# Attention and two MLPs on one core: two sets of query and key buffers in one sequence of all pairs

## The chip, the cores and the metric

The kernel runs on one core of one Trainium2 chip. The metric is device time in microseconds (us); a run's time is that of its one core. The program has five engines with a queue each: TensorE (PE in the profile, its weight loads PEld), VectorE (DVE), ScalarE (ACT), GpSimd (POOL) and SyncE (SP), which issues DMAs.

## The reference

Three parts follow one another, all in fp32. `q`, `k`, `v` have 4 batches, 8 heads, 576 positions of 64 values.

```python
scores = (q @ k.T) / 8, masked where block_i < block_j      # blocks of 64 positions
attn = softmax(scores);  x = (attn @ v), heads side by side    # 2304 tokens x 512
h = x @ w_in1                                                  # 512 -> 2048
g = h if h >= 1, 0 if h <= -1, else (h + 1) ** 2 / 4
x = g @ w_out1                                                 # 2048 -> 512
h = x @ w_in2;  out = (h * cos(h)) @ w_out2                     # the same sizes
```

## The kernel before

**Numbers.** A product in TensorE's float32r keeps fewer bits than fp32, so most operands are split into a high part (`rounded`, line 152, or a ScalarE copy) and the rest (`rest`, line 155), and three products stand for one. Weights are scaled and rounded bit by bit when they come in (`w_convert`, lines 163 to 222), the result is kept in on-chip slots, and all but the first `w_in` are stored to DRAM (`w_store`, line 143) and fetched again when they are next used (`w_fetch`, line 146).

**Attention.** Work goes by pairs of heads, 16 in all (4 batches of 4). A pair has five units, tiles of 128 queries (the last of 64). `load` (line 273) brings K, Q and V of a pair. `prep` (line 296) transposes K or Q on TensorE, in two parts each, and fills the tiles Q, K and L (high parts, low parts, and a zero half). `scores` (line 350) multiplies, takes the maximum on VectorE and the exponential on ScalarE; `scores_tail` (line 406) does so for the last unit. `p_trans` (line 452) transposes the probabilities into PT, `pv` (line 483) multiplies by V. After a pair's last unit its 576 columns go to DRAM (`x1d`, line 528).

**The MLPs.** Tokens go in half-blocks of 512 (the last has 256). For each half-block and layer there are 16 steps, one for each 128 columns of the hidden layer: `mm1` (line 597, 12 products into the PSUM tile `h`), `act` (line 614, the activation as a chain of operations over several engines), and two steps later `mm2` (line 661, 12 products into `a`). The first half-block needs the first batch, the second half-block the second batch too, and so on; `x_load` (line 569) brings x from `x1d`.

**Order.** Functions are generators that yield after every piece of work. `at(d, fn)` puts an operation d ticks later, and a tick passes with every piece (lines 95 to 104). First attention runs alone (`a0`): batch 0 and the first pair of batch 1, with eight PSUM banks and two sets of Q, K, L and of raw K and Q, the second set in a pool `spare`; it divides by the softmax sum after PV (`late`). Then `zipped` (line 758) mixes: for each piece of the MLP it emits `rates` pieces of the remaining 11 pairs (`a1`), for 48 steps, which are three half-blocks of layer 1. There attention has one set of Q, K, L and three PSUM banks, and `h` has one bank; all four `prep` parts of a pair stand ahead of its first unit (line 549), and POOL divides the probabilities. The rest of layer 1 and all of layer 2 follow, with four banks for `h`.

A planner takes these pieces in the order in which they were emitted and sets the order on each engine's queue at build, by a model of the times; on the chip each queue runs in its fixed order, and an instruction that waits holds what is behind it. SP's queue carries every DMA: loads of K, Q, V and weights, stores and fetches of weights, stores and loads of x.

In `load`, K and Q wait for raw tiles that `prep` has read, V for one of two tiles that `pv` has read. Weights of layer 1's `w_out` go round in `RING` = 5 slots.

Of the kernel before, what the change touches and what calls it, by code (L numbers as in the profile page):

```python
# [32 lines left out]
def attn_moe_moe_kernel(ctx: ExitStack, tc: tile.TileContext, q, k, v, w_in1, w_out1, w_in2, w_out2, out):  # L33
    nc = tc.nc
# [30 lines left out]
    one = const.tile([128, 1], F32, name="one")  # L65
# [12 lines left out]
    def consts():  # L78
        make_identity(nc, ident)
        nc.vector.memset(mk_l[:, 0:64], 1.0)  # L80
        nc.vector.memset(mk_l[:, 64:128], 0.0)
        nc.vector.memset(mk_r, 0.0)
        for i, m in enumerate(MASK_PARTS):
            nc.vector.memset(mk_r[32 * i:32 * i + 1, :], m)
        nc.vector.memset(floor_, FLOOR)
        nc.vector.memset(one, 1.0)
        nc.vector.memset(magic, MAGIC)
        nc.vector.memset(hpi, 0.5 * math.pi)
# [54 lines left out]
    def w_store(layer, f, which, t):  # L143
        nc.sync.dma_start(out=wd[layer, f, which], in_=t.rearrange("p a n -> p (a n)").bitcast(F32))
# [86 lines left out]
    def spare(name, shape, dtype):  # L231
        return P.spare.tile(shape, dtype, name=name + "s", tag=name + "s")

    def attn_pools(stack):
        sb = lambda nm, bufs: stack.enter_context(tc.tile_pool(name=nm, bufs=bufs, side="right"))
        P.v, P.pt, P.xs, P.sm = sb("v", 2), sb("pt", 2), sb("xs", 1), sb("sm", 4)
        P.raw, P.p = sb("qkr", 1), sb("p", 3)
        qk = sb("qk", 1)
        own = lambda name, shape, dtype: qk.tile(shape, dtype, name=name)
        P.qk = []  # L240
        for get in (own, spare):
            Q = [get(f"Q{h}", [128, S + 64], F32R) for h in range(2)]
            K = [get(f"K{h}", [128, S], F32R) for h in range(2)]

            L = [get(f"L{h}", [128, S], F32R) for h in range(2)]
# [14 lines left out]
    def attention(pairs, TL, late=False, sets=1):  # L260


        raws, probs, pts, xst, rs, dens = {}, {}, {}, {}, {}, {}
# [6 lines left out]
        def p_tile(u, h):  # L270
            return P.p.tile([128, S], F32, name=f"P{h}", tag=f"P{h}")

        def load(b, p):
            ts = []
            for src, nm in ((k, "rk"), (q, "rq"), (v, "rv")):
                if src is not v and pairs.index((b, p)) % sets == 1:
                    t = spare(nm, [128, NI, 2, D], F32)
                else:
                    t = (P.v if src is v else P.raw).tile([128, NI, 2, D], F32, name=nm, tag=nm)
                for h in range(2):  # L280
                    nc.sync.dma_start(
                        out=t[:, 0:LAST, h, :],
                        in_=src[b, 2 * p + h, 0:128 * LAST, :].rearrange("(t p) d -> p t d", p=128),
                    )
                P.loaded = nc.sync.dma_start(
                    out=t[0:TAIL, LAST], in_=src[b, 2 * p:2 * p + 2, 128 * LAST:S, :].rearrange("h p d -> p h d")
                )
                ts.append(t)
            raws[b, p] = ts
            if sets == 1 or (b, p) != pairs[0]:  # L290
                load_weights(loaded[0] + 1, len(wq) // 2)

        def qk_of(b, p):
            return P.qk[pairs.index((b, p)) % sets]

        def prep(b, p, which, part):
            t = raws[b, p][which]
# [52 lines left out]
        def scores(u, hs):  # L350
# [4 lines left out]
            o = ps_tile()[:, 0:nk * len(hs)].rearrange("p (h n) -> p h n", h=len(hs))  # L355
            qs = slice(128 * i, 128 * i + 128)
            mm = lambda o, l, r, **kw: nc.tensor.matmul(out=o, lhsT=l, rhs=r, skip_group_check=True, **kw)  # L357
            for c, h in enumerate(hs):
                mm(o[:, c], Q[h][:, qs], K[h][:, 0:nk], start=(c == 0), stop=False)
                mm(o[:, c], Q[h][:, qs], L[h][:, 0:nk], start=False, stop=False)  # L360
            for c, h in enumerate(hs):
                mm(o[:, c, nk - 64:nk], mk_l, mk_r, start=False, stop=True)
            if hs[0] == 0:
                dens[u] = [P.sm.tile([128, 2], F32, name=nm, tag=nm) for nm in ("m", "den", "r")]
            m, den, r = dens[u]
            if hs[-1] == 1:
                del dens[u]

            def top():
                nc.vector.tensor_reduce(  # L370
                    out=m[:, hs[0]:hs[-1] + 1], in_=o, axis=AX.X, op=ALU.max, negate=True
                )

            def exp():
                pr = p_tile(u, hs[0])[:, 0:nk * len(hs)].rearrange("p (h n) -> p h n", h=len(hs))
                for c, h in enumerate(hs):
                    probs[u, h] = pr[:, c]
                    e = nc.scalar.activation(  # L378
                        out=pr[:, c], in_=o[:, c], func=ACTF.Exp, bias=m[:, h:h + 1], accum_out=den[:, h:h + 1]
                    )  # L380
                if b == 0:
                    P.act = e

            def norm():
                ds = (0, 1) if late else hs
                if late and hs[-1] == 0:
                    return
                c = slice(ds[0], ds[-1] + 1)
                nc.vector.tensor_scalar(out=den[:, c], in0=den[:, c], scalar1=1e-9, scalar2=None, op0=ALU.add)
                nc.vector.reciprocal(out=r[:, c], in_=den[:, c])  # L390
                for h in ds:
                    if late:
                        rs[u, h] = r[:, h:h + 1]
                        continue
                    pr = probs[u, h]
                    nc.gpsimd.tensor_scalar(  # L396
                        out=pr, in0=pr, scalar1=r[:, h:h + 1], scalar2=1.0, op0=ALU.mult, op1=ALU.mult
# [5 lines left out]

        tails = {}

        def scores_tail(u, c):
# [19 lines left out]
            def exp():  # L426
                pr = p_tile(u, 0)
# [7 lines left out]
            def norm():  # L435
# [5 lines left out]
                if late:  # L441
# [41 lines left out]
        def pv(u):  # L483
            b, p, i = u
            V = raws[b, p][2]
# [16 lines left out]
            if late:  # L502
# [8 lines left out]
            def out_():  # L511
# [4 lines left out]
                if late:  # L516
# [17 lines left out]
        load(*pairs[0])  # L534
        if sets == 2:
            load(*pairs[1])
        yield "loaded"
        two = sets == 2
        for x in range(n + TL + 1):
# [3 lines left out]
            heads = lambda u: [] if u is None else [(0, 1)] if u[2] < 2 else [(0,), (1,)]  # L543
            S_ = [(scores, u, hs) if u[2] < LAST else (scores_tail, u, hs[0]) for hs in heads(u)]
            T_ = [(p_trans, t, hs) for hs in heads(t)]
            V_ = [(pv, w)] if w else []
            pre = []
            if u and u[2] == 0 and (not two or x == 0):
                pre = [(prep, *u[:2], which, part) for which in range(2) for part in range(2)]
            post = []  # L550
            if u and two and 1 <= u[2] <= 4 and pairs.index(u[:2]) + 1 < len(pairs):
                post = [(prep, *pairs[pairs.index(u[:2]) + 1], (u[2] - 1) // 2, (u[2] - 1) % 2)]
            if pre:
                order = pre + T_ + V_ + S_
            else:
                order = S_[:1] + T_[:1] + S_[1:] + T_[1:] + V_ + post
            for fn, *a in order:
                fn(*a)
                yield fn.__name__
# [330 lines left out]
```

## Time and profile before

| what | value |
|---|---|
| median of 3 runs | 1123.7 us (1123.4 to 1125.97) |
| profiled execution | 1123.27 us |
| its span in the profile | 1121.5 us |
| mean granted clock of TensorE | 0.967 |
| busy: PE, PEld, DVE, ACT, POOL | 1052.1, 850.4, 627.6, 560.3, 546.9 us |
| moved by DMA | 200.35 MB, 179 GB/s |

The span runs from the first instruction to the last; the execution's time has 1.8 us more around it. Busy time is the time in which an engine works on an instruction. Attention alone fills the span up to about 84 us, the mix lasts to about 590, the rest of layer 1 to about 730, layer 2 to the end.

### The profile page before, as it was taken

Reading aid. Unit: us, or ns where it says so; the run is one execution under the profiler, and the core shown is the slowest. Engines: PE = TensorE matmul, PEld = TensorE weight load, DVE = VectorE, ACT = ScalarE, POOL = GpSimd, SP = SyncE. Lnnn points to the kernel's source line nnn. Section 1 sums busy time; section 2 is a strip of 40 time slices with the busy share of each in tenths; the row PEclk is TensorE's granted clock in tenths of the full one; section 3 lists DMA queues with packets and bytes.
Section 4 is the critical chain, followed back from the end, with each engine's and each line's share of the span. In section 5 each row is a group of like instructions: output and inputs, shape, how many; then the busy total and the mean of one; then the engine's idle time right before and its main releaser. Section 6 shows DMA issues by size and latency. Waiting matters only on the chain.

```text
span 1121.5 us, 17067 instructions
## 1 busy us (share of the span) xinstructions
PE 1052.1 (94%) x5912; PEld 850.4 (76%) x5912; DVE 627.6 (56%) x1187; ACT 560.3 (50%) x1253; POOL 546.9 (49%) x609
## 2 busy tenths in 40 slices
PE   9988898989999978999959999999999999999998
PEld 7766676666776756777747789978888888888897
DVE  7876848467545376546615653354454454454464
ACT  7887748567545366445524433243343343343343
POOL 2325957577656447648608975322223323322332
PEclk9998998999998997999979999999999999999999
DMA  5687326557636475536794679822542542442353
GB/s 126 179 264 215 116 77 237 183 174 250 204 108 199 124 248 177 193 103 217 266 336 155 222 262 367 324 90 101 170 143 94 167 134 98 150 145 97 113 188 132
DMA packets 144374, 200.35 MB, mean 179 GB/s; under 512 B 65184, under 2 KB 106144, under 8 KB 144288
## 3 DMA queue, kind: packets, MB, share of 16 engines
q1 hardware_dynamic: 144288, 199.26, 53.9%
q8 instruction: 47, 0.77, 0.3%
q14 instruction: 39, 0.32, 0.1%
HBM read 150.47 MB, written 48.76 MB: 178 GB/s over the span
## 4 chain that ended last, share of the span: by engine, by line
PE 42%; POOL 2%; DVE 2%; DMA 2%; ACT 2%; issue 1%; SPq 0%; POOLq 0%; ACTq 0%
PE h L607 20%; PE a L681 17%; PE a L674 4%; DVE gl L155 1%; DMA x2d<-y 1%; DMA x1d<-xs 1%; POOL eb L629 1%; POOL gh L152 1%; POOL w L155 1%; POOL w L152 0%; ACT ea L626 0%; DVE raw L191 0%; DMA raw<-in_moe_w_in_dram 0%; DMA x<-x1d 0%; PE s L463 0%
## 5 line engine op out<-in xcount | busy, mean ns | idle before, releaser
L607 PE MATMUL h<-x,w 128*128 128x512 f32 (+1 forms) x1920 | 445.0, 376 | 18.1 <-DMA x<-x1d 13.7
L607 PEld LDWEIGHTS h<-x,w 128*128 128x128 f32 x1920 | 338.4, 191 | 81.9 <-DMA x<-x1d 14.3
L152 POOL TENSOR_SCALAR gh<-ea 128x512 fp32r<-128x512 f32 (+1 forms) x160 | 100.3, 627 | 256.4 <-DVE ea L654 194.1
L674 PE MATMUL a<-gh,w 128*128 128x512 f32 (+1 forms) x640 | 202.6, 385 | 5.9 <-POOL gh L152 5.9
L629 POOL TENSOR_SCALAR eb<-ea 128x512 f32<-128x512 f32 (+1 forms) x80 | 148.4, 1857 | 62.2 <-ACT ea L626 61.5
L155 DVE TENSOR_TENSOR gl<-ea,gh 128x512 fp32r<-128x512 f32 (+1 forms) x160 | 120.6, 754 | 101.5 <-POOL gh L152 100.8
L681 PE MATMUL a<-w,gh 128*128 128x512 f32 x576 | 174.2, 390 | 0.4 <-POOL gh L152 0.4
L674 PEld LDWEIGHTS a<-gh,w 128*128 128x128 f32 x640 | 119.6, 195 | 26.3 <-POOL gh L152 7.0
L650 ACT ACTIVATE eb<-eb 128x512 f32<-128x512 f32 (+1 forms) x80 | 47.0, 588 | 159.6 <-DVE eb L647 159.6
L674 PE MATMUL a<-gl,w 128*128 128x512 f32 (+1 forms) x320 | 123.1, 387 | 1.5 <-DVE gl L155 1.5
L681 PEld LDWEIGHTS a<-w,gh 128*128 128x128 f32 x576 | 107.1, 188 | 22.2 <-POOL gh L152 0.8
L681 PE MATMUL a<-w,gl 128*128 128x512 f32 x288 | 108.3, 389 | 0.0
L643 POOL TENSOR_SCALAR ea<-ea 128x512 f32<-128x512 f32 (+1 forms) x80 | 65.1, 813 | 75.6 <-ACT ea L640 72.8
L155 POOL TENSOR_TENSOR w<-wv,w 128x512 fp32r<-128x512 f32 x64 | 92.5, 1446 | 10.4 <-ACT w L210 7.1
L626 ACT ACTIVATE ea<-h,one 128x512 f32<-128x512 f32 (+1 forms) x80 | 51.5, 644 | 85.4 <-PE h L607 54.4
L654 DVE TENSOR_TENSOR ea<-h,eb 128x512 f32<-128x512 f32 (+1 forms) x80 | 50.8, 638 | 77.0 <-ACT eb L651 77.0
L640 ACT ACTIVATE ea<-h,magic 128x512 f32<-128x512 f32 (+1 forms) x80 | 51.4, 643 | 74.0 <-PE h L607 59.9
L370 DVE TENSOR_REDUCE m<-s 128x1 f32<-128x384 f32 (+2 forms) x96 | 57.1, 599 | 54.2 <-PE s L357 53.0
L635 DVE SCALAR_TENSOR_TENSOR ea<-ea,eb 128x512 f32<-128x512 f32 (+1 forms) x80 | 61.6, 770 | 43.0 <-ACT eb L632 42.1
L396 POOL TENSOR_SCALAR P<-P,r 128x128 f32<-128x128 f32 (+3 forms) x88 | 61.6, 707 | 48.2 <-DVE r L390 30.8
L191 DVE SCALAR_TENSOR_TENSOR raw<-raw 128x512 uint32<-128x512 uint32 x64 | 49.2, 770 | 64.1 <-ACT raw L182 62.7
L378 ACT ACTIVATE P<-s,m 128x128 f32<-128x128 f32 (+3 forms) x128 | 66.8, 527 | 35.2 <-DVE m L370 35.0
(119 smaller groups left out, 1474.7 us busy)
## 6 DMA issues: line engine op xcount, KB each, us to landing
w<-w2o SPq DMA_DIRECT2D x80, 512.0 KB, 3.2
w<-w1o SPq DMA_DIRECT2D x64, 512.0 KB, 4.5
raw<-in_moe_w_in_dram SPq DMA_DIRECT2D x32, 512.0 KB, 5.6
raw<-in_moe_w_out_dram SPq DMA_DIRECT2D x32, 512.0 KB, 5.1
x1d<-xs SPq DMA_DIRECT2D x16, 576.0 KB, 7.1
x2d<-y SPq DMA_DIRECT2D x36, 256.0 KB, 4.3
x<-x2d SPq DMA_DIRECT2D x36, 256.0 KB, 5.3
w1o<-w SPq DMA_DIRECT2D x16, 512.0 KB, 3.1
```

The lines of the kernel that those rows point to most:

```text
L152: return nc.gpsimd.tensor_scalar(out=hi, in0=raw, scalar1=1.0, scalar2=1.0, op0=ALU.mult, op1=ALU.mult)
L155: (eng or nc.vector).tensor_tensor(out=lo, in0=raw, in1=hi.bitcast(F32), op=ALU.subtract)
L370: nc.vector.tensor_reduce(out=m[:, hs[0]:hs[-1] + 1], in_=o, axis=AX.X, op=ALU.max, negate=True)
L378: e = nc.scalar.activation(out=pr[:, c], in_=o[:, c], func=ACTF.Exp, bias=m[:, h:h + 1], accum_out=den[:, h:h + 1])
L396: nc.gpsimd.tensor_scalar(out=pr, in0=pr, scalar1=r[:, h:h + 1], scalar2=1.0, op0=ALU.mult, op1=ALU.mult)
L607: nc.tensor.matmul(out=hps[s][:, 0:n_], lhsT=w[:, a, kk * 128:(kk + 1) * 128], rhs=x[:, b], start=(kk == 0 and n == 0), stop=(kk == NK - 1 ...
L626: P.act = nc.scalar.activation(out=g, in_=h, func=ACTF.Relu, bias=one)
L629: nc.gpsimd.tensor_scalar(out=u, in0=g, scalar1=2.0, scalar2=0.5, op0=ALU.min, op1=ALU.mult)
L635: nc.vector.scalar_tensor_tensor(out=g, in0=g, scalar=-1.0, in1=u, op0=ALU.add, op1=ALU.max)
L643: nc.gpsimd.tensor_scalar(out=g, in0=g, scalar1=-MAGIC, scalar2=-C1, op0=ALU.add, op1=ALU.mult)
L674: nc.tensor.matmul(out=o, lhsT=w[:, a, dm:dm + 128], rhs=b, start=(f == 0 and n == 0 and c == 0), stop=(f == NF - 1 and n == 2), skip_grou ...
L681: nc.tensor.matmul(out=A, lhsT=b[:, t], rhs=w[:, a, :], start=(f == 0 and n == 0), stop=(f == NF - 1 and n == 2))
```

## The change

- There is one generator `attention(pairs, alone)` for all 16 pairs, with two sets of Q, K and L that are used in turn throughout; raw K and Q have one tile each, and `spare` is gone. `prep` of the next pair is spread over units 1 to 4 of the pair before it, one part each, in the mix too.
- Both heads' scores of a unit are one piece, and in a unit's turn `pv` of three units ago comes first, then the first `p_trans` of two units ago, and so on. PT has one buffer; the probabilities have 3 and 2.
- K, Q and V are loaded by separate calls, K in unit 3 of the pair before the last, Q in unit 0 and V in unit 2, each when its tile has been read.
- Attention runs alone for `START` = 133 pieces, and the same generator goes on in the mix. The first half-block's `x_load` is emitted 20 pieces before the end of the stage. The MLP's pools are opened at the start.
- `w_store` is issued by GpSimd.
- Layer 1's activation is computed as max(min(relu(h/2 + 1/2)², 1), h): the GpSimd operation goes, and the last VectorE operation reads `h` from PSUM. The tile `u` is opened for layer 2 alone.
- `RING` is 6, the rates are 1.2 and 1.06.

```diff
     def w_store(layer, f, which, t):
-        nc.sync.dma_start(out=wd[layer, f, which], in_=t.rearrange("p a n -> p (a n)").bitcast(F32))
+        nc.gpsimd.dma_start(out=wd[layer, f, which], in_=t.rearrange("p a n -> p (a n)").bitcast(F32))
...
-        P.v, P.pt, P.xs, P.sm = sb("v", 2), sb("pt", 2), sb("xs", 1), sb("sm", 4)
-        P.raw, P.p = sb("qkr", 1), sb("p", 3)
+        P.v, P.pt, P.xs, P.sm = sb("v", 2), sb("pt", 1), sb("xs", 1), sb("sm", 4)
+        P.raw, P.p = sb("qkr", 1), [sb("p0", 3), sb("p1", 2)]
...
-        for get in (own, spare):
-            Q = [get(f"Q{h}", [128, S + 64], F32R) for h in range(2)]
+        for c in range(2):
+            get = lambda name, n: qk.tile([128, n], F32R, name=f"{name}{c}")
+            Q = [get(f"Q{h}", S + 64) for h in range(2)]
...
-        load(*pairs[0])
-        if sets == 2:
-            load(*pairs[1])
-        yield "loaded"
+        for which in range(3):
+            load(0, which)
+        for which in range(2):
+            load(1, which)
+        load(1, 2)
+        for part in range(4):
+            prep(*pairs[0], part // 2, part % 2)
+            yield
...
-            pre = []
-            if u and u[2] == 0 and (not two or x == 0):
-                pre = [(prep, *u[:2], which, part) for which in range(2) for part in range(2)]
-            post = []
-            if u and two and 1 <= u[2] <= 4 and pairs.index(u[:2]) + 1 < len(pairs):
-                post = [(prep, *pairs[pairs.index(u[:2]) + 1], (u[2] - 1) // 2, (u[2] - 1) % 2)]
-            if pre:
-                order = pre + T_ + V_ + S_
-            else:
-                order = S_[:1] + T_[:1] + S_[1:] + T_[1:] + V_ + post
+            order = []
+            if w:
+                order.append((pv, w))
+            if u:
+                order += [(scores, u)] if u[2] < LAST else [(scores_tail, u, c) for c in range(2)]
+            if t:
+                order[1:1] = [(p_trans, t, hs) for hs in ([(0, 1)] if t[2] < 2 else [(0,), (1,)])]
+            nx = x // NI + 1
+            if 1 <= x % NI <= 4 and nx < len(pairs):
+                order.append((prep, *pairs[nx], (x % NI - 1) // 2, (x % NI - 1) % 2))
...
-            if u and u[2] == (0 if two else TL):
-                nx = pairs.index(u[:2]) + sets
-                if nx < len(pairs):
-                    at(2, lambda nx=nx: load(*pairs[nx]))
+            which = {3: 0, 0: 1, 2: 2}.get(x % NI)
+            if which is not None and x > 0:
+                at(2, lambda n=x // NI + (2 if which == 0 else 1), which=which: load(n, which))
...
             def s0():
-                P.act = nc.scalar.activation(out=g, in_=h, func=ACTF.Relu, bias=one)
+                P.act = nc.scalar.activation(out=g, in_=h, func=ACTF.Relu, bias=half, scale=0.5)
 
             def s1():
-                nc.gpsimd.tensor_scalar(out=u, in0=g, scalar1=2.0, scalar2=0.5, op0=ALU.min, op1=ALU.mult)
+                nc.scalar.activation(out=g, in_=g, func=ACTF.Square)
 
             def s2():
-                nc.scalar.activation(out=u, in_=u, func=ACTF.Square)
-
-            def s3():
-                nc.vector.scalar_tensor_tensor(out=g, in0=g, scalar=-1.0, in1=u, op0=ALU.add, op1=ALU.max)
+                nc.vector.scalar_tensor_tensor(out=g, in0=g, scalar=1.0, in1=h, op0=ALU.min, op1=ALU.max)
...
-    RING = 5
+    RING = 6
...
-    RATES = (1.3, 1.05)
+    START = 25 * (NP + NX) + 8
+    RATES = (1.2, 1.06)
...
+    a1 = attention([(b, p) for b in range(B) for p in range(NP)], NP + NX)
+    with ExitStack() as st:
...
+        for n in range(START):
+            next(a1)
+            tick()
...
+            if n == START - 20:
+                x_load(steps[0], range(NK))
```

## Rows read from the trace of the kernel before

**Rows 1.** The page's first part: busy time, share and instructions of each engine.

```profile
PE 1052.1 (94%) x5912; PEld 850.4 (76%) x5912; DVE 627.6 (56%) x1187; ACT 560.3 (50%) x1253; POOL 546.9 (49%) x609
```

**Rows 2.** Stretches: length, then busy us of each engine, PEclk, DMA share, GB/s.

```profile
0.00:84.00 84.00, 77.76 (x747) 61.06 (x747) 65.04 (x195) 69.25 (x216) 25.36 (x44) 0.98 0.68 190
84.00:112.00 28.00, 24.11 (x130) 18.71 (x126) 18.30 (x40) 20.44 (x50) 16.59 (x17) 0.88 0.71 216
...
112.00:392.00 280.00, 257.20 (x1468) 197.45 (x1468) 169.36 (x322) 163.73 (x393) 188.37 (x183) 0.96 0.52 167
392.00:448.00 56.00, 45.27 (x279) 33.61 (x278) 36.53 (x77) 36.99 (x97) 32.69 (x42) 0.85 0.67 217
448.00:560.00 112.00, 108.16 (x632) 84.48 (x630) 63.23 (x124) 58.19 (x139) 74.11 (x76) 1.00 0.59 193
560.00:616.00 56.00, 41.76 (x213) 33.25 (x214) 18.28 (x28) 19.29 (x40) 24.35 (x20) 0.85 0.69 246
```

**Rows 3.** The chain in order of time, 560 to 600: start, length, what.

```profile
579.60 8.31 DMA x1d<-xs
...
587.97 2.97 DMA x<-x1d
```

**Rows 4.** TensorE in order of time: start, length, instructions [idle before, released by].

```profile
92.87 1.65 PE L607 MATMUL h<-x,w 128*128 128x512 f32 x3 [1.55 <-DMA x<-x1d]
...
96.35 4.23 PE L607 MATMUL h<-x,w 128*128 128x512 f32 x12
...
344.61 2.69 PE L607 MATMUL h<-x,w 128*128 128x512 f32 x11
...
413.05 0.95 PE L498 MATMUL s<-PT,rv 128*64 128x64 f32 x20
...
431.19 4.09 PE L607 MATMUL h<-x,w 128*128 128x512 f32 x12
...
436.89 1.42 PE L607 MATMUL h<-x,w 128*128 128x512 f32 x5
...
493.38 2.78 PE L607 MATMUL h<-x,w 128*128 128x512 f32 x11
...
572.11 0.33 PE L498 MATMUL s<-PT,rv 64*64 64x64 f32 x4
```

**Rows 5.** TensorE's waits, 112 to 392: for whom, us in total, times, longest.

```profile
PE s L413 <- ACT PT L479: 5.7, 4, 2.4
PE s L463 <- ACT P L378: 3.3, 3, 2.4
PE s L463 <- DVE L L155: 3.1, 3, 2.3
PE a L674 <- POOL gh L152: 2.3, 3, 1.7
PE s L357 <- ACT PT L479: 2.2, 1, 2.2
PE s L305 <- DVE L L155: 1.7, 2, 1.2
```

**Rows 6.** Waits of SP's queue, 0 to 600.

```profile
SPq L144 <- POOL w L155: 106.2, 32, 7.8
SPq L281 <- PE s L498: 62.2, 11, 19.1
```

**Rows 7.** Groups by line: out<-in, count | busy us, mean ns | idle before, releaser.

```profile
L629 POOL TENSOR_SCALAR eb<-ea 128x512 f32<-128x512 f32 (+1 forms) x80 | 148.4, 1857 | 62.2 <-ACT ea L626 61.5
...
L155 POOL TENSOR_TENSOR w<-wv,w 128x512 fp32r<-128x512 f32 x64 | 92.5, 1446 | 10.4 <-ACT w L210 7.1
L626 ACT ACTIVATE ea<-h,one 128x512 f32<-128x512 f32 (+1 forms) x80 | 51.5, 644 | 85.4 <-PE h L607 54.4
L654 DVE TENSOR_TENSOR ea<-h,eb 128x512 f32<-128x512 f32 (+1 forms) x80 | 50.8, 638 | 77.0 <-ACT eb L651 77.0
...
L632 ACT ACTIVATE eb<-eb 128x512 f32<-128x512 f32 (+1 forms) x80 | 47.0, 588 | 52.3 <-POOL eb L629 51.9
```

More of the change, by code (lines that the diff above doesn't have):

```diff
@@ L85, in consts @@
         nc.vector.memset(floor_, FLOOR)
-        nc.vector.memset(one, 1.0)
+        nc.vector.memset(half, 0.5)
         nc.vector.memset(magic, MAGIC)
@@ L258, in attn_moe_moe_kernel, with attention @@
     HALF = S // 2
-    def attention(pairs, TL, late=False, sets=1):
-        raws, probs, pts, xst, rs, dens = {}, {}, {}, {}, {}, {}
+    def attention(pairs, alone):
+        raws, probs, pts, xst, rs, tails = {}, {}, {}, {}, {}, {}
+        TL = 2
+        late = lambda u: pairs.index(u[:2]) < alone
         def ps_tile():
@@ L268, in ps_tile, with load @@
             return pool.tile([128, 512], F32, name="s", tag=tag)
[L270 to L277, printed above, removed]
-                else:
[L279 to L286, printed above, removed]
-                )
-                ts.append(t)
-            raws[b, p] = ts
-            if sets == 1 or (b, p) != pairs[0]:
+        def load(n, which):
+            if n >= len(pairs):
+                return
+            b, p = pairs[n]
+            src, nm = (k, q, v)[which], ("rk", "rq", "rv")[which]
+            t = (P.v if which == 2 else P.raw).tile([128, NI, 2, D], F32, name=nm, tag=nm)
+            for h in range(2):
+                nc.sync.dma_start(
+                    out=t[:, 0:LAST, h, :],
+                    in_=src[b, 2 * p + h, 0:128 * LAST, :].rearrange("(t p) d -> p t d", p=128),
+                )
+            P.loaded = nc.sync.dma_start(
+                out=t[0:TAIL, LAST], in_=src[b, 2 * p:2 * p + 2, 128 * LAST:S, :].rearrange("h p d -> p h d")
+            )
+            raws[b, p, which] = t
+            if which == 2 and 0 < n < alone:
                 load_weights(loaded[0] + 1, len(wq) // 2)
         def qk_of(b, p):
-            return P.qk[pairs.index((b, p)) % sets]
+            return P.qk[pairs.index((b, p)) % 2]
         def prep(b, p, which, part):
-            t = raws[b, p][which]
+            t = raws.pop((b, p, which)) if part else raws[b, p, which]
             tiles = range(0, 2) if part == 0 else range(2, NI)
@@ L382, in exp @@
+                if P.early:
                     P.act = e
             def norm():
[L385 to L392, printed above, removed]
+                nc.vector.tensor_scalar(out=den, in0=den, scalar1=1e-9, scalar2=None, op0=ALU.add)
@@ L393, in norm @@
+                nc.vector.reciprocal(out=r, in_=den)
+                for h in range(2):
+                    if late(u):
                         rs[u, h] = r[:, h:h + 1]
                         continue
-                    pr = probs[u, h]
                     nc.gpsimd.tensor_scalar(
-                        out=pr, in0=pr, scalar1=r[:, h:h + 1], scalar2=1.0, op0=ALU.mult, op1=ALU.mult
+                        out=probs[u, h], in0=probs[u, h], scalar1=r[:, h:h + 1], scalar2=1.0, op0=ALU.mult, op1=ALU.mult
@@ L501, in pv @@
                     )
-            if late:
+            if late(u):
                 for h in range(2):
```

114 lines of the change are left out of this document (47 added, 67 removed).

## The prediction

> **What bounds the kernel now.** The page is read first, for the engine that is never long idle: TensorE is busy 1052.1 of 1121.5 us [rows 1], and the next engine, VectorE, 56%. So a change can only win what TensorE loses, by waiting or by a low clock, and the second view is the table of stretches [rows 2]. Loss there is the length less PE busy, plus busy times (1 minus PEclk). 84–112, the change from attention alone to the mix: 3.9 idle and 2.9 of clock, 6.8 us. 112–392, the mix: 22.8 and 10.3, 33.1. 392–448: 10.7 and 6.8, 17.5. 448–560: 3.8 and 0. 560–616: 14.2 and 6.3, 20.5. Together 81.8. Behind 616 little is lost, and the change hardly touches it. Note 448–560: with the same code and MLP work always at hand, only 3.4% is lost. The reader is to see that the loss sits where the MLP has no x.
>
> Third, the chain in order of time at the worst place [rows 3]: the store of the last pair's attention output was issued at 579.60, landed 8.3 us later, then x was loaded, and only when that had landed, at 590.9, did TensorE go on. This is the MLP waiting for attention. Around 392–448 it is the same: the third batch's attention ends at 414.0 [rows 4], and the third half-block cannot go on before.
>
> Fourth, how late attention is against its place in the program. Counting the yields in the code: `a1` has 275 pieces, the MLP part 280; at the rates 1.3 and 1.05 the last pair is emitted by MLP piece 240 (step 41), the third batch by piece 154 (step 27). The last PV products ran at 572.4, step 41's first ones ended at 496.2: 76 us late. The third batch's last PV ended at 414.0, step 27 was at 344.6: 69 us late [rows 4]. A piece takes at most (560 − 92.87) / 280 = 1.67 us [rows 2, 4]. The x of the next half-block is wanted at pieces 274 and 178, so before has 34 pieces (57 us) and 24 (40 us) in hand, less than the 76 and 69 it is late: the MLP's next half-block comes 20 to 30 us late at each.
>
> **The change part by part.**
>
> *One sequence, emitted earlier.* After has 368 pieces in 16 pairs (23 a pair, since both heads' scores are one piece), and 133 are done alone, 5.8 pairs, against 5. At 1.2 and 1.06 the second batch is emitted by MLP piece 48, the third by 129, the last by 210. Margins: 64 pieces for the last, 49 for the third batch. At 1.5 us a piece (1.67 less the waits) that is 96 and 73 us, against the 76 and 69 that attention is late today. So even if it stays as late, x is there in time, the third batch narrowly; the next two parts should make it less late. I let both stalls go, but for the 3.4% of 448–560 on 56 us each (1.9): 560–616 gives 20.5 − 1.9 = 18.6, 392–448 gives 17.5 − 1.9 = 15.6.
>
> *Two sets of Q, K, L throughout.* Today all four transposes of a new pair come in a lump when the old pair's last scores are done, since there is one set in the mix. TensorE then waits for what fills K and L. Afterwards one part is emitted in each of four units, a pair ahead. TensorE's six longest waits in 112–392 are 18.3 us together [rows 5]; those released by L and gh are 3.1 + 1.7 + 2.3 = 7.1 (gh belongs to the POOL edit below). These 39% go, and I let the same share of the stretch's whole loss go with them: 0.39 × 33.1 = 12.9. The others (PT and P, 5.7 + 3.3 + 2.2 = 11.2) are for one of three PSUM banks or for the softmax; a unit still takes six banks' turns, in another order. Bounds −11.2 (they go) to +11.2 (they double); I take 0.
>
> *x loaded 20 pieces before attention alone ends.* Four DMAs pass SP ahead of some Q, K, V loads that are wanted a unit or more later; SP waits in front of them until the x1d store has landed. Today the first product waits 1.55 us for x [rows 4], after a lump of transposes. I take half of 84–112: 3.4 (bounds 0 and 6.8).
>
> *V loaded when free, weight stores moved to GpSimd.* SP's queue stands 106.2 us for POOL's low weight part before stores, and 62.2 us for V's old reader (PV), and each time the next K, Q, x1d store or x load stands behind it [rows 6]. Both go. None of it is on TensorE's path by itself; it feeds the lateness above, and is counted there. The Trainium skill's "DMA: Bandwidth & Descriptors" (Issuing engines are not separate DMA queues) says that starting DMAs on several engines saves only the starter's issue time. By it only SP's own issue time is won, off the path, and no lateness is cured: the sum would be that of attention coming last, below. The trace differs in this: SP's 106.2 us were spent waiting at the head of the queue, not issuing.
>
> On GpSimd a store is queued behind the low part that the same engine has just written, so it waits for no one. Its price on POOL is shown nowhere: from nothing to POOL's own 1.45 us a weight operation [rows 7], 0 to 70 us for 48 stores; I take the upper, the nearest row. The change also takes 80 × 1.857 = 148.4 us off POOL (the `min`), so POOL, busy 188.37 of 280 in 112–392 [rows 2], gains even then: in the first half-block a step loses one 1.857 and gains one store.
>
> *The shorter layer-1 chain.* Relu and Square stay on ScalarE, the VectorE operation stays and now reads h. So h's only bank in the mix is held for Relu, Square and the VectorE operation, 0.644 + 0.588 + 0.638 (its price from the operation that reads h in layer 2) = 1.87 us, where Relu alone held it 0.644 [rows 7]: 1.23 longer. The next step's products wait for it, and all TensorE work queued behind them. Cover is the twelve products of the step before last, 2.7 us (eleven take 2.69 [rows 4]), and attention. In eight of the 48 steps the next products start under 2.2 us after the last ended; the first is 94.52 to 96.35, the last 435.28 to 436.89 [rows 4]. Lower bound 0, upper 48 × 1.23 = 59; I take 8 × 1.23 = 9.8, since 40 steps have the cover.
>
> *At nothing:* one PT buffer instead of two (PV of the unit before is now emitted ahead of the transposes, so it has read PT when the eviction comes; if planned otherwise, ScalarE waits for a PV, 0.95 [rows 4]); the sixth ring slot; the constant. The 0.8 pair more alone costs the idle of that stage, 84 − 77.76 = 6.2 over five pairs [rows 2], 1.25 × 0.8 = 1.0.
>
> **Sum.** 18.6 + 15.6 + 12.9 + 3.4 = 50.5 gained, 9.8 + 1.0 = 10.8 lost, net 39.7. The profiled execution took 1123.27, 1.8 over its span; against it the sum gives 1083.6. The median of the three runs is 0.4 higher, so 1084.
>
> **The rivals.**
>
> *Everything fits.* With MLP work always at hand, all of 84–616 loses only 3.4%: 81.8 − 0.034 × 532 = 63.7, and h's bank is always covered: 1060. For it: 112 us of just that. Against it: POOL and VectorE are fuller in 112–196, while weights are made.
>
> *Attention still comes last.* If what makes it late grows with the earlier emission (three banks, each with a softmax behind it), the two stalls stay: 50.5 − 34.2 − 10.8 = 5.5 gained, 1118. For it: the third batch's margin of 73 against 69. Against it: its pieces come at the same rate or slower than today. The skill's sentence above points to it.
>
> *h's bank (slower).* Place: the 48 steps of the mix, one h bank. If ScalarE and VectorE reach Square and the last operation late in every step, all of 1.23 is on the path: 1123.7 − 50.5 + 1.0 + 59 = 1133. It decides from (50.5 − 1.0) / 48 = 1.03 us a step on. For it: ScalarE waits for the VectorE maximum and PT evictions in the same queue. Against it: 40 steps with cover.
>
> *It does not do what it says:* each queue's order is planned at build, and the plan may run the MLP ahead of attention anyway, until x runs out in the same places: 1123.
>
> **How the numbers follow.** Forecast 0.62, all fits 0.15, attention last 0.12, h's bank 0.08, no effect 0.03. The forecast's own spread, from the bank waits (±11.2), h's bank and 84–112, is 1066 to 1102. The range 1056 to 1114 takes in the first rival and stops short of the others, leaving out about 0.2. Within 0.3% (3.4 us, about what a measurement here can tell) lie the no-effect case and a part of attention last: 0.06. Slower is h's bank: 0.08. Faster 0.86.
>
> **What would show it.** Right: no wait of TensorE for x over 2 us after the first half-block; the last x1d store issued before the last layer-1 product of the third half-block; the four-transpose lump gone; PEclk at 1.0 where it was 0.85. h's bank would show as a wait of `h` products for the VectorE operation, 1 us or more a step. POOL's busy time should fall by 80 to 130 us. It is wrong if TensorE again waits about 10 us for x near the end of the third half-block, or if idle 112–392 grows.

## The result and the profile after

The changed kernel takes 1114.85 us (1113.45 to 1116.32, 4 runs) against 1124.84 for the kernel before on the same chip, a ratio of 0.991 (95% interval 0.989 to 0.993). It is faster, but by 10 us (0.9%) and not by 40: of the 50.5 us that the prediction counted as gained, most never came.

The stretches of the changed kernel, with the columns and cuts of [rows 2]:

```profile
0.00:84.00 84.00, 73.85 (x646) 56.66 (x646) 59.93 (x175) 60.17 (x190) 21.84 (x42) 0.92 0.60 162
84.00:112.00 28.00, 24.64 (x203) 18.88 (x203) 20.10 (x55) 20.86 (x64) 12.70 (x21) 0.89 0.69 205
112.00:392.00 280.00, 263.26 (x1507) 203.45 (x1506) 175.60 (x308) 176.25 (x416) 134.28 (x177) 0.98 0.58 185
392.00:448.00 56.00, 46.27 (x317) 35.62 (x316) 30.77 (x69) 33.32 (x92) 25.16 (x39) 0.94 0.62 203
448.00:560.00 112.00, 109.21 (x663) 85.35 (x661) 63.07 (x115) 61.33 (x150) 53.53 (x74) 1.00 0.62 208
560.00:616.00 56.00, 41.10 (x172) 33.23 (x173) 26.08 (x31) 18.35 (x31) 22.91 (x26) 0.88 0.74 265
```

Loss is counted as in the prediction: length less PE busy, plus busy times (1 minus PEclk).

| stretch | loss before | after | change | forecast |
|---|---|---|---|---|
| 0–84 | 7.8 | 16.1 | +8.3 | +1.0 |
| 84–112 | 6.8 | 6.1 | −0.7 | −3.4 |
| 112–392 | 33.1 | 22.0 | −11.1 | −12.9 and +9.8 for h's bank |
| 392–448 | 17.5 | 12.5 | −5.0 | −15.6 |
| 448–560 | 3.8 | 2.8 | −1.0 | 0 |
| 560–616 | 20.5 | 19.8 | −0.7 | −18.6 |

The sum is −10.2; the span went from 1121.5 to 1112.7. Each column comes from one execution, so changes of about 1 us say little. The last row is the one to look at: 20 us are lost where they were lost before. The chain of the changed kernel there (start, length, what) is that of [rows 3], 11 to 12 us earlier:

```profile
557.88 9.53 DMA x2d<-y
...
567.50 9.61 DMA x1d<-xs
577.11 0.02 issue
577.12 3.42 DMA x<-x1d
```

TensorE in order of time, changed kernel (start, length, instructions, idle before and releaser), to set beside [rows 4]:

```profile
305.55 3.06 PE L596 MATMUL h<-x,w 128*128 128x512 f32 x12
...
408.13 0.95 PE L488 MATMUL s<-PT,rv 128*64 128x64 f32 x20
...
451.74 3.02 PE L596 MATMUL h<-x,w 128*128 128x512 f32 x12
...
559.05 0.95 PE L488 MATMUL s<-PT,rv 128*64 128x64 f32 x20 [0.32 <-ACT PT L467]
...
580.68 1.62 PE L596 MATMUL h<-x,w 128*128 128x512 f32 x3 [13.91 <-DMA x<-x1d]
```

The last row is what the prediction named as its refutation: TensorE waits 13.9 us for x. The others say why. Lines 1 and 3 are the first products of steps 22 and 36 (counted from 0, as in the code), beside which the third and the last batch were emitted; lines 2 and 4 are their last PV products. Attention now runs 103 and 105 us behind its place in the emission (409.1 less 305.6, and 560.0 less the 454.8 at which step 36's products end), where it was 69 and 76 late before. It was emitted 25 and 30 pieces earlier, 37 and 45 us at 1.5 us a piece, and became 34 and 29 us later against that place: most of what was gained on paper.

TensorE's waits, 112 to 392, changed kernel, against [rows 5]:

```profile
PE h L596 <- DVE ea L621: 7.5, 7, 1.6
PE s L488 <- ACT P L418: 4.4, 1, 4.4
PE s L488 <- ACT P L373: 2.4, 4, 1.7
PE s L463 <- ACT P L373: 0.9, 1, 0.9
```

In this stretch nothing waits for L or gh any more. In their place stands the new chain's VectorE operation, which holds h's bank.

### The profile page after: what moved, and what is told of

Its sections match the earlier page's. It is cut to its first block, busy times and chain, and to the rows that moved or that the text cites. A ratio compares the mean times of both kernels' runs of the same rounds, so it can differ in the third digit from the quotient of the medians.

```text
span 1112.7 us, 17002 instructions
## 1 busy us (share of the span) xinstructions
PE 1046.3 (94%) x5912; PEld 847.5 (76%) x5912; DVE 618.3 (56%) x1143; ACT 558.6 (50%) x1253; POOL 410.8 (37%) x577
## 4 chain that ended last, share of the span: by engine, by line
PE 72%; ACT 8%; DMA 8%; DVE 6%; issue 3%; SPq 2%; POOL 1%; POOLq 0%; ACTq 0%; DVEq 0%
PE h L596 32%; PE a L667 17%; PE a L660 12%; PE s L488 4%; DMA raw<-in_moe_w_in_dram 3%; PE s L350 3%; PE s L451 2%; DMA x1d<-xs 2%; ACT raw L182 2%; ACT raw L176 2%; ACT P L373 1%; PE s L299 1%; DVE wv L195 1%; DMA w2i<-w 1%; DVE raw L191 1%
## 5 line engine op out<-in xcount | busy, mean ns | idle before, releaser
L596 PE MATMUL h<-x,w 128*128 128x512 f32 (+1 forms) x1920 | 439.4, 377 | 28.1 <-DMA x<-x1d 13.9
L660 PE MATMUL a<-gh,w 128*128 128x512 f32 (+1 forms) x640 | 199.7, 376 | 0.0
L660 PEld LDWEIGHTS a<-gh,w 128*128 128x128 f32 x640 | 116.0, 189 | 18.3 <-issue 0.7
L615 ACT ACTIVATE ea<-h,half 128x512 f32<-128x512 f32 (+1 forms) x80 | 51.6, 644 | 141.4 <-PE h L596 134.6
L155 POOL TENSOR_TENSOR w<-wv,w 128x512 fp32r<-128x512 f32 x64 | 87.5, 1369 | 13.1 <-ACT w L210 11.2
L488 PE MATMUL s<-PT,rv 128*64 128x128 f32 (+2 forms) x960 | 73.8, 274 | 16.5 <-ACT P L418 6.1
L632 DVE TENSOR_TENSOR eb<-h,ea 128x512 f32<-128x512 f32 (+1 forms) x80 | 51.0, 637 | 57.3 <-POOL ea L629 57.3
L373 ACT ACTIVATE P<-s,m 128x512 f32<-128x512 f32 (+3 forms) x128 | 66.5, 524 | 31.2 <-DVE m L366 30.0
L621 DVE SCALAR_TENSOR_TENSOR ea<-ea,h 128x512 f32<-128x512 f32 (+1 forms) x80 | 50.4, 630 | 54.9 <-ACT ea L618 54.0
L488 PEld LDWEIGHTS s<-PT,rv 128*64 128x64 f32 (+1 forms) x960 | 50.5, 140 | 39.1 <-issue 10.6
```

Source lines behind the costliest of these rows:

```text
L155: (eng or nc.vector).tensor_tensor(out=lo, in0=raw, in1=hi.bitcast(F32), op=ALU.subtract)
L373: e = nc.scalar.activation(out=probs[u, h], in_=os[h], func=ACTF.Exp, bias=m[:, h:h + 1], accum_out=den[:, h:h + 1])
L488: nc.tensor.matmul(out=ps[64 * h:64 * h + 64, 0:nq], lhsT=V[0:n, j, h, :], rhs=r, start=(j == 0), stop=(j == i), skip_group_check=True,)
L596: nc.tensor.matmul(out=hps[s][:, 0:n_], lhsT=w[:, a, kk * 128:(kk + 1) * 128], rhs=x[:, b], start=(kk == 0 and n == 0), stop=(kk == NK - 1 ...
L615: P.act = nc.scalar.activation(out=g, in_=h, func=ACTF.Relu, bias=half, scale=0.5)
L632: nc.vector.tensor_tensor(out=u, in0=h, in1=g, op=ALU.add)
```

## Experiments

Each ratio is against runs of the kernel before taken beside it, whose median was 1126 to 1129 us. "Pace" is the time from one pair's last PV to the next, over the last ten pairs: 41.2 us before (160.1 to 572.4), 42.1 in the changed kernel (139.0 to 560.0). The last PV products of the sixth pair, from which it is counted, in the kernel before, the changed kernel, the run with four banks and its control (below):

```profile
159.18 0.95 PE L498 MATMUL s<-PT,rv 128*64 128x64 f32 x20
...
138.03 0.95 PE L488 MATMUL s<-PT,rv 128*64 128x64 f32 x20
...
121.83 0.95 PE L488 MATMUL s<-PT,rv 128*64 128x64 f32 x20
...
131.45 0.95 PE L488 MATMUL s<-PT,rv 128*64 128x64 f32 x20
```

**Does the place in the emission set where attention runs?** It was the prediction's own premise.

```diff
-    RATES = (1.2, 1.06)
+    RATES = (2.0, 2.0)
```

> The changed kernel with attention emitted much earlier: 2.0 attention pieces per MLP piece in place of 1.2 and 1.06, nothing else. Rival (emission order sets where attention runs, as the prediction assumed): the last pair's output is stored 40 us or more before the MLP wants it, the 14 us wait for x near 580 goes, time 1085 to 1100. Theory (the banks set the pace, the emission only queues up): last PV still at 555 to 562, the wait for x still 12 to 15 us, time 1113 to 1117.

Measured: 1114.2, ratio 0.989 (0.985 to 0.992); last PV at 558.6, and this wait:

```profile
579.44 2.90 PE L596 MATMUL h<-x,w 128*128 128x512 f32 x6 [14.04 <-DMA x<-x1d]
```

Emitting attention still earlier has no effect: the last PV moves by 1.4 us and the wait stays. What holds attention back is something else. (Slower rates were not tried.)

**A fourth bank, and its control.** Both leave out the MLP's fourth accumulator; only the first gives its bank to attention, the control has the second edit without the first. Not shown are the flags and the stores that go with the second edit, and that the stage alone has three spare banks for four in both. With its own banks and h's that stage has eight banks in the run with four, and seven in the control.

```diff
-        P.ps = [(stack.enter_context(tc.tile_pool(name="ps_s", bufs=3, space=PSUM, side="right")), "s")] * 3
+        P.ps = [(stack.enter_context(tc.tile_pool(name="ps_s", bufs=4, space=PSUM, side="right")), "s")] * 4
...
-            acc[s[:2], part] = M.a.tile([128, 512], F32, name=f"a{part}", tag=f"a{part}")
+            acc[s[:2], part] = acc[s[:2], 2] if part == 3 else M.a.tile([128, 512], F32, name=f"a{part}", tag=f"a{part}")
```

> The changed kernel, but attention gets four PSUM banks in the mix in place of three. To free the bank, the MLP's fourth accumulator is left out: its products are added into the third's bank (same number of products, same stores; those output columns are wrong), and the stage of attention alone gets three spare banks, not four. Theory (attention's pace in the mix is set by the turns of its three banks, each held through softmax or eviction): pace falls from 42 us a pair to 36 or less, both waits for x (12 us at 392-448, 20 us at 560-616) mostly go, and the time is 1075 to 1095. Rival 1 (the place of the work, by the emission rates, sets the pace): no change, 1110 to 1118. Rival 2 (TensorE in the mix is simply full, so attention can only go faster at the cost of the MLP): the waits go but 112-392 grows or the MLP slows by the same, 1105 to 1115.

> The control of the run with four banks: the MLP's fourth accumulator is left out in the same way (its products are added into the third's bank, those output columns are wrong), but attention keeps three banks in the mix. Theory (the fourth attention bank, not the missing accumulator, gave the 52 us): 1108 to 1118, with both waits for x back. Rival (leaving out an accumulator is itself the gain): 1062 to 1075.

Measured: 1062.5 with four banks (ratio 0.943, 0.939 to 0.947), 1101.5 for the control (0.977, 0.975 to 0.980). So the bank is worth 39 us. Little of that is made in the stage alone, where the control is a bank short: the MLP's first product runs at 105.2 and 106.7 us. The stretches with four banks, from 112 on:

```profile
112.00:392.00 280.00, 276.83 (x1709) 215.32 (x1710) 190.38 (x357) 194.94 (x483) 164.14 (x210) 1.00 0.64 202
392.00:448.00 56.00, 55.47 (x341) 43.28 (x340) 35.26 (x72) 36.20 (x89) 27.72 (x41) 1.00 0.73 243
448.00:560.00 112.00, 108.33 (x559) 85.93 (x557) 51.62 (x80) 46.85 (x97) 48.52 (x60) 0.98 0.74 252
560.00:616.00 56.00, 56.00 (x271) 47.30 (x270) 27.00 (x39) 22.14 (x38) 26.01 (x31) 1.00 0.74 250
```

and those of the control:

```profile
112.00:392.00 280.00, 266.56 (x1566) 207.39 (x1565) 176.14 (x321) 183.45 (x434) 143.03 (x186) 0.98 0.61 195
392.00:448.00 56.00, 50.93 (x299) 38.63 (x298) 31.30 (x65) 32.25 (x85) 25.38 (x41) 0.88 0.63 188
448.00:560.00 112.00, 102.17 (x624) 80.20 (x622) 54.68 (x102) 55.19 (x135) 49.58 (x64) 0.99 0.69 237
560.00:616.00 56.00, 49.07 (x206) 40.16 (x207) 30.67 (x38) 23.03 (x38) 32.01 (x35) 0.90 0.64 225
```

From 112 to 616 the loss is 9.5 us with four banks and 52.7 with three. The last PV of the third and the last batch with four banks, then that of the last in the control:

```profile
349.94 0.95 PE L488 MATMUL s<-PT,rv 128*64 128x64 f32 x20
...
488.45 0.95 PE L488 MATMUL s<-PT,rv 128*64 128x64 f32 x20
...
521.46 5.80 PE L596 MATMUL h<-x,w 128*128 128x512 f32 x18 [2.40 <-DMA x<-x1d]
...
545.78 0.95 PE L488 MATMUL s<-PT,rv 128*64 128x64 f32 x20 [0.32 <-ACT PT L467]
```

The third batch ends at 351 and the last pair at 489, a pace of 36.7 us (control 41.4), and x is there but for 2.4 us (13.4 in the control). TensorE is then busy 98.9% of 112–392 at a granted clock of 1.00, so more banks could win little there. A unit takes three to six turns of a bank, each held through a maximum, an exponential or an eviction; with three banks attention gets about one unit through in a step of the MLP (a pace of 42 us is 8.4 a unit; a step takes about 9.2), TensorE is filled with MLP products, and these run ahead until x is out. The Trainium skill's "Perfetto Trace Analysis" (Identifying Performance Opportunities) says that gaps which repeat can mean too little PSUM for the next tile; this trace bears that out only in part, since here the shortage shows as one long wait for x at the end of a half-block.

The control is 13 us faster than the changed kernel, though its wait for x is as long, which I can't explain.

**Can the bank be had without leaving anything out?** h's bank is idle for much of a step, so every fourth attention tile took it, with the new and with the old layer-1 chain.

```diff
         flush()
-        P.ps = own
+        P.ps = own + [(M.h[0], "h")]
```

> The changed kernel whole, nothing left out; in the mix every fourth attention tile takes h's bank, which the MLP step leaves free between its products, so attention turns over four banks, one of them lent. Theory (attention's pace is its banks' turns): last pair done by step 44, no wait for x, 1070 to 1095; the price is that h's products now also wait for attention's evictions. Rival (h's bank is the tighter of the two, since the new chain holds it longer): h's products wait 1 us or more in each of the 48 steps and the time is 1110 to 1140.

> As the run before, with the old layer-1 chain, which gives h's bank back after Relu (ring of five for want of SBUF). Theory: shorter hold of the lent bank, so 5 to 15 us below that run: 1060 to 1085. Rival (GpSimd's 148 us of min and multiply are then on the path of gh): equal to it or slower by up to 10.

Measured: 1238.5 (ratio 1.098) and 1141.2 (1.011). TensorE's waits, 112 to 560, in the first:

```profile
PE s L350 <- DVE ea L621: 11.4, 6, 2.8
PE s L451 <- DVE ea L621: 11.2, 5, 4.7
PE s L488 <- DVE ea L621: 8.9, 4, 3.3
```

Both are far outside what was expected. Attention's products now wait for the MLP's activation: the lent bank ties both streams together, where one of attention's own helped. The three rows are 31.5 us of the 124 that the first run lost; its granted clock also fell, to 0.84 in 112–392, and the pace to 51.9 us. The old chain, which gives h back after Relu, makes this 97 us cheaper.

**More pairs alone.** With a fixed pace, a pair taken out of the mix should make all later ones early. 31 stands for 6.8 pairs; 54 and 77, for 7.8 and 8.8, were run too.

```diff
-    START = 25 * (NP + NX) + 8
+    START = 25 * (NP + NX) + 31
-            if n == START - 20:
+            if n == 113:
```

> The changed kernel with one more pair done in the stage of attention alone (6.8 pairs in place of 5.8); the first x is loaded where it was. Theory (attention runs at a fixed pace of 42 us a pair in the mix, so each pair taken out of the mix makes the rest early): the MLP starts about 17 us later (first product at 125), the last pair ends 20 to 25 us earlier against the MLP, and both waits for x (in all about 25 us of the loss) fall to under 8 us. The pair alone costs about 2 to 3 us of idle and low clock. Time 1095 to 1107. Rival (emission or SP queue sets the lateness): the waits stay, time 1114 to 1120.

> The changed kernel with two more pairs done in the stage of attention alone (7.8 in place of 5.8), first x loaded where it was. One more pair gave 5 us and left a wait of 11.2 us for x. Theory (a fixed pace of 42 us or more a pair in the mix): the last pair now ends by step 46, the wait for x goes, and the MLP's start moves from 134 to about 151; 1092 to 1103. Rival (what is gained at the end is paid for by the stage alone, whose loss is 3 us a pair, and by the MLP's low clock later): 1106 to 1112.

> The changed kernel with 8.8 pairs alone in place of 5.8 (7.8 gave 27 us below the changed kernel). Theory (once no wait for x is left, a pair more alone only costs): last pair ends by step 40, the MLP works by itself from there, and each pair alone loses 2 to 3 us; 1087 to 1093, that is the same or up to 6 slower than with 7.8. Rival (less attention in the mix also shortens the waits in the mix by more than that): 1078 to 1086.

Measured: 1109.6 (0.984), 1086.9 (0.964, 0.959 to 0.970) and 1095.2 (0.971). With 7.8 pairs the last one ends at 529.9, step 48 begins at 538.1, and there is no wait for x. With 8.8 the time is some 8 us longer. With 6.8 the last pair ends at 556.0, only 4 us earlier than in the changed kernel, and 11.2 us of the wait are left, so too much was expected of it. For the pace is not fixed: from the first pair wholly in the mix to the last it is 41.7 us with 5.8 pairs alone, and 44.8, 45.1 and 45.3 with more, with the same three banks. What slows it then, no run shows.

**The new chain.**

```diff
-                P.act = nc.scalar.activation(out=g, in_=h, func=ACTF.Relu, bias=half, scale=0.5)
+                P.act = nc.scalar.activation(out=g, in_=h, func=ACTF.Relu, bias=half)
...
-                nc.scalar.activation(out=g, in_=g, func=ACTF.Square)
+                nc.gpsimd.tensor_scalar(out=u, in0=g, scalar1=2.0, scalar2=0.5, op0=ALU.min, op1=ALU.mult)
...
-    RING = 6
+    RING = 5
```

> The changed kernel with the old layer-1 activation chain (GpSimd's min and multiply back, VectorE's last operation reads SBUF and not h's bank; ring of five for want of SBUF). Forecast in the prediction: h's bank, held 1.23 us longer, costs 9.8 us. By that the kernel is faster without the new chain where TensorE is full, but POOL gets 148 us of work back: 1105 to 1115, and the waits of h's products for VectorE (9.9 us in all) go to under 3. Rival (what GpSimd was relieved of is what made 112-392 better by 11 us): 1118 to 1126.

> The changed kernel with the ring of output weights at five slots as before, not six: the control of the run with the old layer-1 chain, which had five too. Theory (the chain, not the ring, made that run 12.6 us faster): 1112 to 1118. Rival (six slots cost the time, for instance by loads that collide): 1100 to 1106.

> As the run before with the old layer-1 chain (ring of five). Theory (the two gains add: 12 us of the chain, 12 to 20 of the earlier place): 1080 to 1092. Rival (both act on the same wait for x): 1095 to 1102.

> The kernel before with the new layer-1 chain alone (the rest of the change left out). By the run of the changed kernel with the old chain (12.6 us faster than with the new one) the new chain alone costs time: 1130 to 1138 (+6 to +14). Rival (the prediction's: GpSimd's relief in 112-392 at least pays for h's bank): 1113 to 1124.

Measured: the changed kernel with the old chain 1102.2 (0.979, 0.974 to 0.984), its control with five slots 1111.1 (0.986, 0.981 to 0.990). With 7.8 pairs alone the old chain (five slots) is 16 us slower than the new (six; 1102.7 against 1086.9), outside both ranges: the wait for x, which the new chain has lost there, is back with 13.4 us. The new chain alone on the kernel before gives 1123.3 (0.994, 0.991 to 0.997). The waits of h's products for VectorE go with the old chain (no such row from 84 to 600), but the new chain costs 9 us in one place and is worth 16 and 5 in the two others. Since every edit makes the planner lay all queues anew, I put no difference under some 10 us down to one edit alone.

**The stage alone.** First the second PT buffer (`sb("pt", 1)` becomes 2, not shown), against the control with five slots; then also the order in a unit, shown here, against the run with two buffers; and last the changed kernel's order alone, put into the kernel before.

```diff
-            if w:
-                order.append((pv, w))
             if u:
                 order += [(scores, u)] if u[2] < LAST else [(scores_tail, u, c) for c in range(2)]
             if t:
-                order[1:1] = [(p_trans, t, hs) for hs in ([(0, 1)] if t[2] < 2 else [(0,), (1,)])]
+                order += [(p_trans, t, hs) for hs in ([(0, 1)] if t[2] < 2 else [(0,), (1,)])]
+            if w:
+                order.append((pv, w))
```

> The control above with two buffers for the transposed probabilities, as before the change. TensorE waited 3.9 us for their eviction in 0-112 of the changed kernel, and the stage of attention alone takes 17.0 us a pair in place of 15.1. Theory (the single buffer is what slows the stage alone): the last product of the fifth pair ends at 90 to 94, not 98.7, the first MLP product starts 5 to 8 us earlier, time 5 to 8 us below the control. Rival (the order of the pieces, products ahead of scores, slows it): the fifth pair still ends at 97 to 99, time within 3 us of the control.

> The control with two buffers for the transposed probabilities, and each unit's pieces in the order of the kernel before: scores, transposes of the probabilities, PV products, in place of PV, transposes, scores. Theory (the order slows the stage alone): the fifth pair's last product ends at 88 to 92, not 96.9, time 4 to 8 us below that control. Rival (it is something else, as the 0.8 pair more or the clock): still 95 to 98, time within 3 us.

> The kernel before with one thing of the change alone: in each unit PV first, then the transposes, then the scores, as the changed kernel has it. Theory (this order costs by itself): the fifth pair's last product ends 3 to 8 us later than 87.2, time 1132 to 1145. Rival (it costs only with one PT buffer and two sets throughout): 1120 to 1130.

Measured: 1109.0 (0.983, 0.978 to 0.988) with two PT buffers, no difference from its control; 1090.3 (0.965, 0.960 to 0.970) with the scores first as well, 18.6 us less, more than was expected. The fifth pair ends at 99.2 in the changed kernel, 98.1 in the control, 97.3 with two buffers, 92.9 with the scores first. Two stretches with the scores first, then the second of them with PV first and two buffers:

```profile
0.00:84.00 84.00, 77.76 (x707) 60.99 (x707) 65.07 (x193) 66.12 (x208) 25.84 (x48) 0.94 0.64 172
...
392.00:448.00 56.00, 51.17 (x286) 38.96 (x286) 30.58 (x65) 31.23 (x81) 24.77 (x36) 0.88 0.58 180
...
392.00:448.00 56.00, 43.82 (x277) 33.81 (x278) 30.87 (x66) 30.91 (x85) 21.57 (x35) 0.82 0.56 173
```

In 0–84 the idle with the scores first is 6.2 us, that of the kernel before, against 10.2 in the changed one. As I read it, PV first puts the scores, which have the longest way before them (maximum, exponential, transposes), at the end of each unit. Most of the 18.6 lies at 392–448, whose loss is 11.0 against 20.1 with PV first and two buffers; the long wait for x is still there, 11.1 us for 13.6. In the kernel before the same order costs 5.5 us in 0–84 (13.3 for 7.8) and the fifth pair ends at 91.6, but the time doesn't grow (1124.3, ratio 0.996): what was lost alone is given back before x is wanted.

**SP's queue.** In one run weight stores are back on SP (the first pair of lines), in another K, Q and V are loaded by GpSimd (the second).

```diff
-        nc.gpsimd.dma_start(out=wd[layer, f, which], in_=t.rearrange("p a n -> p (a n)").bitcast(F32))
+        nc.sync.dma_start(out=wd[layer, f, which], in_=t.rearrange("p a n -> p (a n)").bitcast(F32))
...
-                nc.sync.dma_start(
+                nc.gpsimd.dma_start(
```

> The changed kernel with the weight stores issued by SP again. Theory (banks set the pace; the SP queue is not on the path): time within 4 us of the changed kernel, 1111 to 1119, wait for x still 12 to 15 us. Rival (the prediction's: SP standing at the head of stores feeds the lateness): 1120 to 1130, and loads of K, Q, V land late, seen as TensorE waiting for a DMA of rk, rq or rv.

> The changed kernel with the loads of Q, K and V issued by GpSimd, so that SP's queue holds only weights, x and stores. Theory (banks): 1111 to 1119, the same. Rival (loads that wait in SP's queue for their buffer hold up the x1d store and the x load behind them): the chain of store and load before the wait for x shortens, wait under 10 us, 1105 to 1111.

Measured: 1114.2 (0.988, 0.983 to 0.992), the same as the changed kernel; and 1134.6 (1.006), 20 us slower than it and outside both ranges. The first settles that moving the stores bought nothing. That agrees with the Trainium skill's "DMA: Bandwidth & Descriptors" (Issuing engines are not separate DMA queues), by which only the starter's own time is saved: a store's issue takes GpSimd 0.60 us. The second is no clean test: weights that stood behind the first loads in SP's queue now start at 0.7 us, and K's tiles land after 6.9 us, not 3.3. From 0 to 112 it loses 40 us for 22, and its wait for x is 13.5, so the last x is no sooner there.

**All repairs together**: scores first, two PT buffers, five slots, 7.8 pairs alone.

> The changed kernel with the three repairs together: scores first in a unit, two buffers for the transposed probabilities (ring of five), 7.8 pairs alone. Theory (they add): scores first gave 18.6 us against its control, of which some 2.5 were already the wait for x; 7.8 pairs alone gave 27: 1066 to 1078, no wait for x over 2 us. Rival (both mend the same loss): 1080 to 1090.

Measured: 1076.7 (1071.8 to 1079.6, 6 runs), ratio 0.953 (0.950 to 0.957), with nothing left out of the computation. It beats both kernels, by 4.7% and some 4%. A wait of 2.8 us for x is left. The gains add in part: in full they would give 1114.9 − 28.0 − 18.6 = 1068.3. Its stretches from 392:

```profile
392.00:448.00 56.00, 53.22 (x301) 41.17 (x300) 32.50 (x62) 32.03 (x77) 25.81 (x36) 0.97 0.75 244
448.00:560.00 112.00, 104.26 (x550) 81.37 (x550) 50.27 (x81) 47.76 (x103) 51.80 (x64) 0.97 0.73 254
560.00:616.00 56.00, 56.00 (x249) 46.37 (x248) 30.50 (x44) 25.18 (x43) 33.33 (x38) 1.00 0.77 258
```

## Why the prediction was wrong

**The step that failed** is the first: "even if it stays as late, x is there in time". The margins (73 and 96 us) were worked out rightly, but lateness is no property of attention that stays. It is the difference between a place on paper and where a pace of some 42 us a pair brings attention, so emitting 37 and 45 us earlier made it 34 and 29 us larger. The runs: rates of 2.0 change nothing, and a fourth bank takes the pace from 41.4 to 36.7 us and gives 39 us. The two stalls were to give 34.2 and gave 5.7. The rival "attention still comes last" had this mechanism (three banks, each with a softmax behind it), this place and nearly this time, 1118; it was given 0.12, because "its pieces come at the same rate or slower than today" was read as evidence against it, when the pace of 41.2 us a pair in the trace of before spoke for it. The banks are not the whole of the pace, as the runs with more pairs alone show.

**Undersized:** the stage alone, 1.0 forecast, 8.3 found. Only the 0.8 pair more was priced; the new order in a unit was taken at nothing. Of the 8.3, 3.9 are idle and 4.4 a lower granted clock (0.92 for 0.98). The clock part is uncertain: with the same stage alone it was 0.90 with rates of 2.0 and 0.96 with five slots, and the stretch lost 18.0 and 14.5 for the 16.1 of the changed kernel. With the scores first again the idle is back at 6.2 and the clock at 0.94. The single PT buffer, also taken at nothing, is not the cause.

**Came, but not taken apart:** two sets of Q, K and L, 12.9 forecast for 112–392, from which most of h's 9.8 was to be taken; 11.1 came net, 6.1 of idle and 5.0 of clock. The lump of transposes and the waits for L are gone, but no run has the two sets alone, and the lighter GpSimd acts in the same stretch. POOL's busy time fell by 136, a little more than the 80 to 130 forecast: a store costs GpSimd 0.60 us, not up to 1.45. **Small:** 84–112 gave 0.7 of 3.4. (The prediction's losses add up to 81.7, not 81.8, which changes nothing.)

**Right by luck:** h's bank. TensorE waits for the new VectorE operation 9.8 us from 84 to 600, by forecast 9.8. The forecast took eight steps whose next products start under 2.2 us after the last ended; in the changed kernel none of the first 47 does, the shortest such time is 3.5 us. The waits fall elsewhere, since the bank is held longer than the 1.87 us added up: from a step's last product to the end of the VectorE operation it is 2.2 to 7.9 us, half of the time over 3.7. Both engines have other work ahead in their queues. In step 20, for one, the products end at 292.3, Relu (line 615) starts at 294.2, and the VectorE operation (line 621) ends at 298.0:

```profile
291.61 0.71 PE L596 MATMUL h<-x,w 128*128 128x512 f32 x2
...
294.17 0.68 ACT L615 ACTIVATE ea<-h,half 128x512 f32<-128x512 f32 x1
...
297.30 0.67 DVE L621 SCALAR_TENSOR_TENSOR ea<-ea,h 128x512 f32<-128x512 f32 x1
...
298.02 1.20 PE L596 MATMUL h<-x,w 128*128 128x512 f32 x4 [1.64 <-DVE ea L621]
```

Whether that reaches the time, the runs leave open.

**SP's queue** was held to feed the lateness. With the stores back on SP the pace and the wait stay (42.0 us a pair, 13.2 us in all). It has a part at one place: the last pair's output is ready on VectorE at 561.8 and its store is issued at 567.5, behind six weight fetches. SP in order of time, changed kernel and, last, the longest row of SP's waits from 560 to 568:

```profile
556.90 2.41 SPq L691 DMA_DIRECT2D x2d<-y  x4
560.47 6.93 SPq L148 DMA_DIRECT2D w<-w2i  x6
567.50 0.38 SPq L518 DMA_DIRECT2D x1d<-xs  x1
...
SPq L148 <- DMA raw<-in_moe_w_in_dram: 2.2, 2, 1.1
```

That is 5.7 of the 20.7 us from the last PV to the next product; store and load take 13.0 to land. The fetches wait mostly for older DMAs to land, and so does the store: by the chain shown with the result it goes when the x2d store issued at 557.88, the eighth DMA before it on SP, has landed at 567.41. In this trace SP never has more than eight DMAs under way, and here each takes about 9 us to land. Whether the chip or the program's way of issuing sets the eight, no run shows.

**Open:** the 13 us of the control without the fourth accumulator, the sign of the new chain, and what besides the banks sets the pace.

## What to carry over

When one stream runs late behind another on the same engine, first find what its pace is per item and which buffer's turns make it; a margin counted from the order of emission holds only if that order is what holds it back. Emitting earlier moved nothing that waits for a buffer, while another private bank moved the last pair by 57 us, and two pairs fewer in the stage where the bank is short by 30. The order of a unit's pieces is an edit with a price: here the order that starts the longest chain first was 18.6 us cheaper.

## Not expected of the hardware

Transfers took longer to land where more ran beside them. The last x1d store took 9.6 us (the chain above); the first, of the same size, 4.3. DMA issues of the changed kernel, 0 to 40 (count, KB each, median us to landing):

```profile
rk<-in_k_dram SPq DMA_DIRECT2D x8, 128.0 KB, 3.3
...
x1d<-xs SPq DMA_DIRECT2D x1, 576.0 KB, 4.3
```

In 560–616 the DMAs move 265 GB/s, in 0–84 162.
